# Batch 0 by token slot, its u made transposed in PSUM, and three-chunk weight pieces in a gated-recurrence and mixer kernel

## The chip, the cores and the metric

The kernel runs on one core of one Trainium2 chip. The metric is device time in microseconds (us) of one execution, lower is better; the time before is the median of three runs.

## The reference

Two parts follow one another. The first is a recurrence per batch and head over 768 tokens, with a state of 48 by 48; its output, with heads side by side, is x of 768 tokens by 384 channels. The second is a mixer: two matmuls over tokens with a residual give u, two matmuls over channels with a residual give the output.

```python
B, H, S, D = 4, 8, 768, 48
for t in range(S):
    state = alpha[:, :, t, :, None] * state + einsum('bhd,bhe->bhde', k[:, :, t], v[:, :, t])
    y[:, :, t] = einsum('bhd,bhde->bhe', q[:, :, t], state)
x = y.transpose(0, 2, 1, 3).reshape(B, S, H * D)                 # 4, 768, 384
h = maximum(x.transpose(0, 2, 1) @ w_tok1, 0) @ w_tok2           # w_tok1 768 x 256, w_tok2 256 x 768
u = x + h.transpose(0, 2, 1)
out = u + maximum(u @ w_ch1, 0) @ w_ch2                          # w_ch1 384 x 1536, w_ch2 1536 x 384
```

All inputs and the output are float32; the kernel computes in bf16 with float32 sums in PSUM.

## The kernel before

**Attention.** Each batch is cut into three blocks of 256 tokens, numbered 0 to 11 over the four batches. A partition holds two neighbouring tokens of a block (the two token slots), so that one load per block and tensor (alpha, k, q, v) brings 384 KB in rows of 384 bytes. For a block, `ln` and cumulative sums on TensorE (`cum`, or `cumw` in blocks 0 to 2) and exponentials on ScalarE (`E`, `IE`) give decay factors; `kk` and `qq` scale k and q by them; `trk`/`trq` with `evk`/`evq` transpose them (through TensorE in blocks 0 to 5, through DMA transposes `dk` and `dq` in blocks 6 to 11). `G0_`, `G1_` are the score products of the two halves of 128 tokens, `mask0_`, `mask1_` mask them on VectorE into `gtm`, `K` is the product of k and v for the state, `s`, or `sa` and `sm`, update the state, `ia`/`ib` add the state's part to the output, `y` the part within the block, and `x0_`, `x1_` copy the result to x. Two of these steps need whole halves of 128 tokens on the partitions, so that `vs0_`, `vs1_`, `ka`, `kb` and `kc` copy 64 partitions each across the two slots. A second form of the block, by token slot, is in the code and unused (`SLOT = ()`): `gslot` and `maskslot` go by slot, `khalf` and `yslot` use 64 rows of the TensorE array at a time, and `kadd` adds the old state in PSUM by an identity matmul. It needs none of the five copies.

**Mixer.** Per batch: `t1` (12 matmuls of 384 columns) and `ht` (ReLU) are the first token layer, `t2` (12 matmuls) the second; `u` adds x on VectorE. The channel layers need u transposed (`ut`): batch 0 transposes on TensorE (`UP = (0,)`, operations `up` and `ut`), batches 1 to 3 by two DMA transposes `ux`. `c1` (72 matmuls, with ReLU `rt`) and `c2` (72 matmuls in 24 groups) are the channel layers, `o` adds u on VectorE, and `st` stores.

**Weights** come in 16 loads of 384 KB (`ldw`) and are cast to bf16 (`cw`): two pieces of w_tok1 (`wt1`), two of w_tok2 (`wt2`, 128 rows each), six of w_ch1 (`wc1`: 128 rows by 768 columns), six of w_ch2 (`wc2`). `c1` with the first six groups of 128 columns needs three `wc1` pieces, with the last six the other three.

**Order.** Nothing is scheduled on the chip by chance: a search with a cost model, run beforehand, left a written list (`ORDER`) of some 930 operations. The last letter of each is its engine: t TensorE, v VectorE (DVE), s ScalarE (ACT), g GpSimd (POOL), y SyncE (SP), the queue that issues all loads and DMA transposes. Each engine works through its operations in the list's order, so an operation that waits holds up all behind it on its engine. `BUFS` are the buffer numbers that belong to it. Operations named f1 to f12 are fillers: matmuls on zeros, in units of 512 columns, put where TensorE would wait. [...]

Around the change the list of before reads, from the last block of batch 0 to the first channel matmul (`c1_0_11_0`):

```
ia2t y0_2t x0_2s t1_0_0_1t t1_0_0_2t E3s t1_0_0_3t mask1_2v t1_0_1_3t ib2t y1_2t ldw_wc14y t1_0_1_4t
x1_2s t1_0_0_4t f1_t1_0_1_5t t1_0_1_5t ht_0_1v P4g cw_wt21s t1_0_0_5t ht_0_0s f3_t2_0_0t t2_0_0t t2_0_1t u_0_0v ln13s
r13s ldw_wc13y t2_0_2t u_0_1v t2_0_3t u_0_2v t2_0_5t lnP4s t2_0_4t u_0_3v u_0_5v u_0_4v up_0_0t cw_wc14s cw_wc13s
ldw_wc15y up_0_1t ld_qt3y k0a3g kk3g cum4t trk3t cw_wc15g ut_0_0v up_0_2t ut_0_2v ut_0_1s c1_0_11_0t c1_0_8_0t IE4s
```

Of the kernel before, what the change touches and what calls it, by code (L numbers as in the profile page):

```python
# [9 lines left out]
BF16 = mybir.dt.bfloat16  # L10
# [84 lines left out]
B, H, S, D = 4, 8, 768, 48  # L95
# [6 lines left out]
UP = (0,)  # L102
# [11 lines left out]
SLOT = ()  # L114
# [6 lines left out]
def build(g):  # L121
# [194 lines left out]
    def mixer(b):  # L316
# [27 lines left out]
        uts = []
        if b in UP:
            for p in range(3):
                bank = V("one")
                o = P.op(f"up_{b}_{p}", pe([128] * 6), m0 + (3900 + 340 * p) * sc, writes=[bank],
                         reads=list(dict.fromkeys([us[2 * p][0], us[2 * p + 1][0]])),
                         preds=[us[2 * p][1], us[2 * p + 1][1]],  # L350
                         emit=lambda e, p=p, bank=bank: g.utr(bank, [us[2 * p][0], us[2 * p + 1][0]], p))
                uts.append(P.op(f"ut_{b}_{p}", either(dve(768, True), act(768)), m0 + (3950 + 340 * p) * sc, writes=[ut],
                                reads=[bank], preds=[o], emit=lambda e, p=p, bank=bank: g.utev(e, ut, bank, p)))
        else:
            for half in range(2):
                uts.append(P.op(f"ux_{b}_{half}", {"SP": (1240.0, 1240.0)}, m0 + (3900 + 500 * half) * sc, writes=[ut],
                                reads=[us[3 * half][0]], preds=[us[3 * half + i][1] for i in range(3)],
                                emit=lambda e, half=half: g.uxbar(ut, us[3 * half][0], half),
                                dma=("x", 1450.0, 1180.0, 480.0)))
        rts = []  # L360
        for mc in range(NDC):
            rt = V("rt")
            ro = []
            for half in range(2):
                bank = V("one")
                o = P.op(f"c1_{b}_{mc}_{half}", pe([384] * 3), m0 + (4900 + 975 * mc + 487 * half) * sc, writes=[bank],
                         reads=[ut], preds=(uts[0:2 + half] if b in UP else [uts[half]]) + [wl[("wc1", p)] for p in ((0, 1, 2) if mc < 6 else (3, 4, 5))],
# [5 lines left out]
        for i in range(NS):  # L373
            hold = 4000.0 if (i >= NS - 3 and b < B - 1) else 0.0
            cuts = [(0, HD // 2), (HD // 2, HD)] if (b, i) == LAST else [(0, HD)]
            for ci, (ca, cz) in enumerate(cuts):
# [3 lines left out]
                for q4 in range(4):  # L380
                    pp = []
                    for mc in range(3 * q4, 3 * q4 + 3):
# [6 lines left out]
                          reads=[bank, us[i][0]], preds=[prev],  # L389
# [20 lines left out]
ld_at1y ld_at0y ln1s ln0s f8_cumw1t f1_cumw1t cumw1t IE1s cumw0t IE0s ld_vt0y E0s vb0g vs0_0g vs1_0v ld_kt0y kk0v  # L410
f8_trk0t f1_trk0t trk0t E1s ld_qt0y qq0v ka0s kb0s kc0v f1_trq0t trq0t ld_kt1y kk1v K0t evq0s s0_0v ld_vt1y vb1s
f1_trk1t trk1t ld_at2y evk0v ln2s f2_G0_0t G0_0t ld_qt1y ka1g sa1_0v f4_cumw2t cumw2t mask0_0v vs0_1s kb1g kc1g vs1_1s
K1t sm1_0g qq1v sa0_1v sm0_1v G1_0t ld_kt2y IE2s E2s trq1t evq1s ib0t mask1_0v f3_y1_0t y1_0t y0_0t evk1v G0_1t sa1_1v
ld_qt2y x1_0s mask0_1v G1_1t ld_vt2y x0_0s vb2s kk2g trk2t kc2s ldw_wt10y qq2g cw_wt10s f2_ia1t ia1t mask1_1v evk2s
trq2t ld_at3y vs1_2g ldw_wt11y evq2v ib1t y1_1t y0_1t vs0_2g ldw_wt21y sm1_1g P3g K2t sa0_2v sm0_2g x0_1s t1_0_0_0t
f1_G0_2t G0_2t ldw_wt20y G1_2t cw_wt20g t1_0_1_0t mask0_2v x1_1s t1_0_1_1t ld_at4y ld_kt3y t1_0_1_2t lnP3s cum3t
cw_wt11s IE3s ia2t y0_2t x0_2s t1_0_0_1t t1_0_0_2t E3s t1_0_0_3t mask1_2v t1_0_1_3t ib2t y1_2t ldw_wc14y t1_0_1_4t
x1_2s t1_0_0_4t f1_t1_0_1_5t t1_0_1_5t ht_0_1v P4g cw_wt21s t1_0_0_5t ht_0_0s f3_t2_0_0t t2_0_0t t2_0_1t u_0_0v ln13s
r13s ldw_wc13y t2_0_2t u_0_1v t2_0_3t u_0_2v t2_0_5t lnP4s t2_0_4t u_0_3v u_0_5v u_0_4v up_0_0t cw_wc14s cw_wc13s
ldw_wc15y up_0_1t ld_qt3y k0a3g kk3g cum4t trk3t cw_wc15g ut_0_0v up_0_2t ut_0_2v ut_0_1s c1_0_11_0t c1_0_8_0t IE4s  # L420
c1_0_11_1t rt_0_8_0v rt_0_11_0v ldw_wc11y q0r3g qq3g c1_0_9_1t rt_0_9_1v ln14s kb3s c1_0_10_0t cw_wc11s c1_0_9_0t
rt_0_9_0v rt_0_11_1v E4s c1_0_7_0t c1_0_10_1t c1_0_7_1t ldw_wc10y r14s cw_wc10s rt_0_10_1v trq3t evk3s rt_0_7_0v
ldw_wc12y ld_vt3y cw_wc12g c1_0_2_0t c1_0_0_1t ka3g rt_0_7_1s c1_0_8_1t rt_0_10_0v vb3v vs1_3g vs0_3g rt_0_0_1v
rt_0_2_0v evq3s ld_at5y ld_qt4y c1_0_1_1t rt_0_8_1v c1_0_3_0t kc3s K3t P5g c1_0_4_1t rt_0_3_0s rt_0_1_1s q0r4g G0_3t
ld_kt4y qq4g s0_3v ln15s G1_3t sa1_3v c1_0_2_1t rt_0_2_1s mask0_3v lnP5s c1_0_1_0t c1_0_5_1t rt_0_5_1s rt_0_1_0s r15s
mask1_3v ldw_wc21y cw_wc21s k0a4g ldw_wc20y c1_0_6_1t rt_0_6_1v c1_0_4_0t kk4v ldw_wc22y c1_0_5_0t c1_0_0_0t cw_wc22s
rt_0_4_0v rt_0_0_0v cw_wc20g rt_0_4_1s c1_0_6_0t rt_0_6_0v c1_0_3_1t trq4t rt_0_3_1v cum5t trk4t ld_kt5y k0a5g
ldw_wc23y rt_0_5_0s c2_0_3_0t c2_0_5_0t evq4s kb4s evk4v ld_qt5y G1_4t mask1_4v G0_4t ld_vt4y c2_0_0_0t IE5s c2_0_0_1t
ka4g cw_wc23s c2_0_3_1t kc4s sm1_3g E5s mask0_4v ib3t y1_3t ldw_wc24y cw_wc24s c2_0_5_1t vb4g vs1_4s x1_3s ia4t
ldw_wc25y vs0_4g cw_wc25s ld_at6y y0_3t kk5v c2_0_3_2t y0_4t q0r5v trk5t evk5s qq5v K4t c2_0_0_2t sa0_4v c2_0_0_3t P6v  # L430
x0_3s ld_at7y sm0_4g o_0_0v trq5t x0_4s sa1_4v P7g evq5s lnP6s c2_0_5_2t c2_0_5_3t ld_vt5y vb5g c2_0_4_0t c2_0_4_1t
ld_kt7y kc5g G1_5t G0_5t lnP7s o_0_5v ib4t y1_4t vs1_5s mask1_5v t1_1_1_0t t1_1_1_1t sm1_4g x1_4s c2_0_4_2t c2_0_3_3t
vs0_5s ld_at8y t1_1_1_2t st_0_5s K5t mask0_5v sa0_5v sm0_5v cum6t t1_1_0_0t ld_kt6y k0a6g t1_1_0_1t ld_qt6y c2_0_2_0t
ln17s ld_qt7y ia5t y0_5t x0_5s IE6s kk6g ib5t y1_5t ln16s E6s t1_1_0_2t x1_5v t1_1_0_3t t1_1_1_3t cum7t E7s o_0_3v
t1_1_1_4t t1_1_1_5t r16s ld_kt8y q0r6g ld_vt6y dk6y P8g ht_1_1v lnP8s t1_1_0_4t t1_1_0_5t c2_0_2_1t c2_0_2_2t ln18s
ht_1_0v t2_1_1t u_1_1v t2_1_2t t2_1_0t t2_1_4t u_1_2v u_1_0v ux_1_0y c2_0_1_0t c2_0_1_1t vb6s IE7s qq6v r17s t2_1_3t
# [529 lines left out]
```

## Time and profile before

| | us |
|---|---|
| three runs | 163.32, 163.56, 162.62 |
| median | 163.32 |
| span of the profiled execution, first to last instruction | 160.5 |
| TensorE busy (matmuls) | 154.6 |
| VectorE, ScalarE, GpSimd busy | 114.9, 97.8, 80.8 |

The profiled execution has no time of its own beside its span; the median of the runs lies 2.8 us above that span. In the profile PE is TensorE's matmul side, PEld its weight loads, DVE, ACT and POOL the Vector, Scalar and GpSimd engines, SPq the issuing queue of SyncE. Matmuls are pipelined: a single one of 384 columns is shown with 0.33 us, a row of them advances by about half of that each. In rows of the timeline the first number is the start in us from the first instruction, the second the duration, and a bracket tells the idle time ahead and what ended it; in groups stand busy us and mean ns.

### The profile page before, as it was taken

What the parts mean: (1) busy time and instruction counts of PE and PEld (TensorE: products, weight loads), DVE (VectorE), ACT (ScalarE), POOL (GpSimd) and SP (SyncE); (2) the same over time, 40 slices, a digit from 0 to 9 for tenths busy, and PEclk for the clock granted to TensorE, in tenths of its full rate; (3) what the DMA queues carried; (4) which work ended last, traced back from release to release, by engine and by line L of the source; (5) the groups of instructions that cost most, each with busy time, mean ns of one, the idle gap of its engine ahead of it and who ended that gap; (6) DMA issues with size and microseconds to landing.
All of it is one profiled execution on the core that took longest, in us unless ns stands there. A gap on an engine that the chain in (4) does not pass through costs nothing.

```text
span 160.5 us, 3971 instructions
## 1 busy us (share of the span) xinstructions
PE 154.6 (96%) x1563; PEld 97.1 (60%) x1563; DVE 114.9 (72%) x206; ACT 97.8 (61%) x179; POOL 80.8 (50%) x94
## 2 busy tenths in 40 slices
PE   7999989999999999999999999999999999999992
PEld 2545565766667676666667666566567665665661
DVE  6099994979889787989969758795886762464222
ACT  3789999998899955897563583269832203343000
POOL 5205897695973649389778852699523000000000
PEclk9999999999999999999999999999999999999999
DMA  4999999999999999999989999989701235111133
GB/s 122 320 324 317 317 374 311 339 333 306 316 347 324 275 278 272 210 228 319 241 202 298 239 315 204 217 196 134 196 21 62 87 79 169 49 49 53 49 129 116
DMA packets 76130, 35.05 MB, mean 218 GB/s; under 512 B 70352, under 2 KB 74320, under 8 KB 76112
## 3 DMA queue, kind: packets, MB, share of 16 engines
q1 hardware_dynamic: 73808, 31.76, 74.1%
q10 hardware_dynamic: 2304, 3.05, 5.3%
q8 instruction: 12, 0.20, 0.5%
q14 instruction: 6, 0.05, 0.1%
HBM read 25.17 MB, written 4.72 MB: 186 GB/s over the span
## 4 chain that ended last, share of the span: by engine, by line
PE 61%; DMA 12%; DVE 6%; ACT 6%; SPq 6%; POOL 4%; issue 3%; DVEq 0%; POOLq 0%
PE ps L907 22%; PE ps L902 21%; PE ps L643 11%; DMA in<-in_v_dram 6%; SPq L584 6%; DMA out_dram<-o 4%; PE ps L878 3%; PE ps L883 2%; DMA ut<-u 2%; DVE pkk L700 2%; DVE gtm L770 1%; PE ps L712 1%; DVE rt L875 1%; POOL vb L746 1%; POOL pkq L700 1%
## 5 line engine op out<-in xcount | busy, mean ns | idle before, releaser
L907 PE MATMUL ps<-wc,rt 128*128 128x384 bf16 (+1 forms) x300 | 52.4, 319 | 0.0
L902 PE MATMUL ps<-ut,wc 128*128 128x384 bf16 x288 | 50.3, 326 | 0.1
L902 PEld LDWEIGHTS <-wc 128*128 128x128 bf16 x288 | 27.1, 98 | 17.9 <-DMA ut<-u 0.6
L907 PEld LDWEIGHTS <-rt 128*128 128x128 bf16 x300 | 27.8, 98 | 16.0
L873 ACT ACTIVATE rt<-ps 128x384 bf16<-128x384 f32 x47 | 21.4, 492 | 23.6 <-PE ps L902 23.3
L875 DVE TENSOR_SCALAR rt<-ps 128x384 bf16<-128x384 f32 x49 | 25.6, 551 | 9.1 <-PE ps L902 8.9
L770 DVE TENSOR_TENSOR gtm<-ps,mk 128x1024 bf16<-128x1024 f32 x24 | 28.5, 1218 | 3.1 <-PE ps L643 2.8
L911 DVE TENSOR_TENSOR o<-ps,u 128x384 f32<-128x384 f32 (+1 forms) x25 | 13.2, 536 | 12.6 <-PE ps L907 10.1
L700 POOL TENSOR_TENSOR pkk<-in,IE 128x768 bf16<-128x768 f32 x8 | 14.5, 1817 | 3.3 <-DVE ss L844 2.3
L745 ACT CAST x<-ps 128x384 bf16<-128x384 f32 x20 | 9.2, 479 | 11.1 <-PE ps L643 9.5
L887 DVE TENSOR_TENSOR u<-ps,x 128x384 bf16<-128x384 f32 x24 | 12.0, 550 | 3.1 <-PE ps L883 2.5
L746 POOL CAST vb<-in 64x384 bf16<-64x384 f32 (+1 forms) x14 | 8.3, 594 | 10.4 <-DMA in<-in_v_dram 4.7
L692 POOL TENSOR_TENSOR in<-in,in 128x384 f32<-128x384 f32 x8 | 8.0, 1000 | 10.5 <-DVE u L887 3.8
L643 PE MATMUL ps<-rt 128*128 128x512 bf16 (+1 forms) x29 | 12.1, 515 | 1.1 <-DVE rt L541 1.1
L745 ACT CAST vb<-in 64x384 bf16<-64x384 f32 (+1 forms) x18 | 11.4, 634 | 0.8 <-DMA in<-in_v_dram 0.3
L700 POOL TENSOR_TENSOR pkq<-in,E 128x768 bf16<-128x768 f32 x6 | 10.9, 1818 | 0.6 <-DMA tpk<-pkq 0.3
L878 PE MATMUL ps<-x,wt 128*128 128x384 bf16 x48 | 11.0, 325 | 0.0
L844 POOL TENSOR_TENSOR ss<-tmp,E 128x384 bf16<-128x384 f32 x10 | 8.3, 833 | 4.2 <-DVE in L628 3.9
L841 DVE TENSOR_TENSOR tmp<-ps,ss 128x384 f32<-128x384 f32 x16 | 8.8, 552 | 1.8 <-PE ps L643 0.6
L883 PE MATMUL ps<-ht,wt 128*128 128x384 bf16 x48 | 9.1, 326 | 0.0
L643 PE MATMUL ps<-vb,gtm 128*128 128x48 bf16 x192 | 8.2, 183 | 0.2 <-DVE gtm L770 0.2
L643 PE MATMUL ps<-tpq,tpk 48*64 48x128 bf16 (+1 forms) x288 | 7.9, 218 | 0.4 <-POOL tpq L746 0.3
(94 smaller groups left out, 207.6 us busy)
## 6 DMA issues: line engine op xcount, KB each, us to landing
in<-in_alpha_dram SPq DMA_DIRECT2D x12, 384.0 KB, 5.1
in<-in_v_dram SPq DMA_DIRECT2D x12, 384.0 KB, 5.6
in<-in_k_dram SPq DMA_DIRECT2D x12, 384.0 KB, 5.2
in<-in_q_dram SPq DMA_DIRECT2D x12, 384.0 KB, 5.5
in<-in_moe_w_ch_dram SPq DMA_DIRECT2D x12, 384.0 KB, 5.9
out_dram<-o ACTq DMA_DIRECT2D x15, 192.0 KB, 1.8
in<-in_moe_w_tok_dram SPq DMA_DIRECT2D x4, 384.0 KB, 6.0
out_dram<-o SPq DMA_DIRECT2D x8, 192.0 KB, 2.2
```

Source lines behind the costliest of these rows:

```text
L643: return self.pe.matmul(out, lhsT=lhsT, rhs=rhs, start=start, stop=stop, skip_group_check=True)
L700: self.shared(self.eng[e].tensor_tensor(self.t(dst)[:, :, h0:h1, 0:D], self.t(src)[:, h0:h1].rearrange("p h s d -> p s h d"), bass.AP(tens ...
L745: return self.act.copy(d, s)
L770: self.nc.vector.tensor_tensor(self.t(gtm)[:, hf, :, :], self.pair(gp).rearrange("p a (j t) -> p (a j) t", t=128), bass.AP(tensor=m.tensor ...
L873: self.act.activation(d, s, AF.Relu)
L875: self.nc.vector.tensor_scalar_max(d, s, 0.0)
L878: self.pe.matmul(self.bank(bank)[:, 0:HD], lhsT=self.wt1[:, kc, m * 128 : m * 128 + 128], rhs=self.t(x), start=(kc == 0), stop=(kc == NS - 1))
L883: self.pe.matmul(self.bank(bank)[:, 0:HD], lhsT=self.wt2[:, kc, i * 128 : i * 128 + 128], rhs=self.t(hts[kc]), start=(kc == 0), stop=(kc = ...
L887: self.nc.vector.tensor_tensor(self.t(u)[:, i % 3], self.bank(bank)[:, 0:HD], self.t(x), ALU.add)
L902: self.pe.matmul(self.bank(bank)[:, 0:HD], lhsT=self.wc1[:, kc, mc * 128 : mc * 128 + 128], rhs=self.t(ut)[:, 3 * half : 3 * half + 3, kc, ...
L907: self.pe.matmul(self.bank(bank)[:, 0 : cz - ca], lhsT=self.t(rts[mc][0])[:, i * 128 : i * 128 + 128], rhs=self.wc2[:, mc, ca:cz], start=( ...
L911: self.nc.vector.tensor_tensor(self.t(o)[:, ca:cz], self.bank(bank)[:, 0 : cz - ca], self.t(u)[:, i % 3, ca:cz], ALU.add)
```

## The change

1. `SLOT = (0,1,2)`: the three blocks of batch 0 use the form by token slot. The copies `ka`, `kb`, `kc`, `vs` of these blocks go, and their state additions are made by TensorE (`A`).
2. `UDIR = (0,)` in place of `UP`: batch 0's second token layer is computed transposed (`tt`), after identity matmuls (`xa`) have put x, transposed, into the same PSUM bank; six copies (`ut`) of 384 columns give ut directly. u in its natural layout, which `o` needs, comes back from ut by two DMA transposes on the SP queue (`un_0_1`, `un_0_0`).
3. Weight pieces: a `wc1` piece is now all 384 rows by 256 columns, so that a channel group needs one piece; a `wt2` piece is all 256 rows by 384 columns. Each load still moves 384 KB; its rows are 1,024 and 1,536 bytes long in place of 3,072.
4. `ORDER` and `BUFS` are new as a whole, for all batches. Fillers go from 36 units to 27.

```diff
-UP = (0,)
+UP = ()
+UDIR = (0,)
-SLOT = ()
+SLOT = (0,1,2)
...
+        if b in UDIR:
+            ut, us, uts = V("ut"), [], []
+            for half in range(2):
+                evs = []
+                for j in range(NM):
+                    bank = V("one")
+                    tx = x[3 * half : 3 * half + 3]
+                    xa = P.op(f"xa_{b}_{half}_{j}", pe([128] * 3), ..., writes=[bank],
+                              reads=[v for v, _ in tx], preds=[o for _, o in tx], ...)
+                    o = P.op(f"tt_{b}_{half}_{j}", pe([384] * 2), ..., writes=[bank],
+                             reads=[h for h, _ in hts], preds=[h for _, h in hts] + [xa, wl[("wt2", half)]], ...)
+                    evs.append(P.op(f"ut_{b}_{half}_{j}", either(act(384), dve(384)), ...,
+                                    writes=[ut], reads=[bank], preds=[o], ...))
+                uts.append(evs)
                 u = V("u")
+                un = P.op(f"un_{b}_{half}", {"SP": (1240.0, 1240.0)}, m0 + 6000 * sc, writes=[u], reads=[ut], preds=evs,
+                          emit=lambda e, u=u, half=half: g.unat(u, ut, half), dma=("x", 1450.0, 1180.0, 480.0))
+                us += [(u, un)] * 3
...
-                         ... [wl[("wc1", p)] for p in ((0, 1, 2) if mc < 6 else (3, 4, 5))],
+                         ... [wl[("wc1", mc // 2)]],
...
-                          reads=[bank, us[i][0]], preds=[prev],
+                          reads=[bank, us[i][0]], preds=[prev, us[i][1]],
...
-            self.gated(dma(t, self.w[1][128 * piece : 128 * piece + 128, :]), op)
+            w = self.w[1].rearrange("(c p) m -> p c m", p=128)
+            self.gated(dma(t.rearrange("p (c m) -> p c m", c=2), w[:, :, HD * piece : HD * piece + HD]), op)
         elif nm == "wc1":
-            c, h = piece % 3, piece // 3
-            self.gated(dma(t, self.w[2][128 * c : 128 * c + 128, 768 * h : 768 * h + 768]), op)
+            w = self.w[2].rearrange("(c p) m -> p c m", p=128)
+            self.gated(dma(t.rearrange("p (c m) -> p c m", c=3), w[:, :, 256 * piece : 256 * piece + 256]), op)
...
+    def xadd(self, bank, xs, j):
+        for i, x in enumerate(xs):
+            self.mm(self.bank(bank)[:, i * 128 : i * 128 + 128], self.t(x)[:, j * 128 : j * 128 + 128], self.idn, i == 0, False)
+
+    def tok2t(self, bank, half, j, hts):
+        for kc in range(NDT):
+            self.mm(self.bank(bank)[:, 0:HD], self.t(hts[kc])[:, j * 128 : j * 128 + 128],
+                    self.wt2[:, half, kc, :], False, kc == NDT - 1)
+
+    def utev3(self, e, ut, bank, half, j):
+        self.copy(e, self.t(ut)[:, 3 * half : 3 * half + 3, j, :], self.bank(bank)[:, 0:HD].rearrange("p (i t) -> p i t", i=3))
+
+    def unat(self, u, ut, half):
+        self.nc.sync.dma_start_transpose(self.t(u).rearrange("p i (j c) -> p (i j) c", j=NM),
+                                         self.t(ut)[:, 3 * half : 3 * half + 3].rearrange("p i j t -> p (i j t)"))
```

The new list, in the two places that the prediction follows: from the scores of the last block of batch 0 to the first channel matmul (`c1_0_4_1`), and from the last channel weights to batch 1's second token layer (`t2_1_0`). Loads leave in the list's order; `ldw_wc12` is the 20th, `ldw_wc24` the 39th, `ld_at7` the 43rd.

```
ld_qt2y G0_1t x0_0s mask0_1v ld_kt2y ld_vt2y qq2g f3_trq2t trq2t evq2s ldw_wt10y A1_1t s1_1v G1_1t mask1_1v kk2g
ld_at3y ln13s f2_trk2t trk2t ia1t evk2v f2_G1_2t G1_2t mask1_2v P3g ib1t y1t cw_wt10s r13s lnP3s G0_2t ia2t mask0_2v
vb2g K2t A0_2t x0_1s x1_1s cum3t IE3s ldw_wt20y cw_wt20g t1_0_1_0t t1_0_1_1t s0_2v E3s xa_0_0_1t ib2t y2t t1_0_0_0t
t1_0_1_2t x0_2v ld_at4y P4g lnP4s ldw_wt11y x1_2s ln14s r14s ld_qt3y t1_0_0_1t cw_wt11g t1_0_1_3t t1_0_0_2t t1_0_0_3t
q0r3v qq3v t1_0_1_4t ldw_wt21y xa_0_0_2t t1_0_1_5t ht_0_1s t1_0_0_4t t1_0_0_5t xa_0_1_1t ht_0_0s cum4t cw_wt21v trq3t
evq3v tt_0_1_1t xa_0_1_0t tt_0_1_0t ut_0_1_0s ut_0_1_1s xa_0_0_0t IE4s xa_0_1_2t tt_0_1_2t ut_0_1_2v ldw_wc12y
tt_0_0_0t ut_0_0_0s cw_wc12g ld_kt3y k0a3g kk3v tt_0_0_1t tt_0_0_2t ut_0_0_1v c1_0_4_1t rt_0_4_1v c1_0_5_1t ld_at5y
...
x1_4v G0_5t ldw_wc23y G1_5t cw_wc23g mask1_5v mask0_5v ldw_wc24y cw_wc24g c2_0_5_2t c2_0_2_2t ldw_wc25y c2_0_3_1t
sm1_4g K5t sa0_5v sm0_5v ld_at8y P8g ld_kt7y cw_wc25s c2_0_2_3t un_0_1y c2_0_3_2t ld_at7y P7v ia5t y0_5t x0_5s
t1_1_0_0t t1_1_0_1t c2_0_5_3t o_0_5v ld_at6y ld_kt6y ib5t y1_5t t1_1_1_2t x1_5s t1_1_0_2t t1_1_1_3t P6g t1_1_0_3t
t1_1_0_4t t1_1_1_4t t1_1_1_5t ld_qt6y t1_1_0_5t c2_0_4_0t c2_0_4_1t ht_1_0v ln17s lnP7s ld_kt8y ld_vt7y ht_1_1s
t2_1_0t u_1_0v ln16s t2_1_2t t2_1_5t cum7t t2_1_1t u_1_5v u_1_1v k0a7g u_1_2v c2_0_3_3t r16s q0r6v IE7s kk7g lnP6s
```

More of the change, by code (lines that the diff above doesn't have):

```diff
@@ L366, in mixer @@
                 o = P.op(f"c1_{b}_{mc}_{half}", pe([384] * 3), m0 + (4900 + 975 * mc + 487 * half) * sc, writes=[bank],
-                         reads=[ut], preds=(uts[0:2 + half] if b in UP else [uts[half]]) + [wl[("wc1", p)] for p in ((0, 1, 2) if mc < 6 else (3, 4, 5))],
+                         reads=[ut], preds=(uts[half] if b in UDIR else uts[0:2 + half] if b in UP else [uts[half]]) + [wl[("wc1", mc // 2)]],
                          emit=lambda e, mc=mc, half=half, bank=bank: g.ch1(bank, ut, mc, half))
@@ L415 @@
[L415 to L424, printed above, removed]
@@ L613, in wcast @@
         elif nm == "wt2":
-            d = self.wt2[:, piece, :]
+            d, t = self.wt2[:, piece], t.rearrange("p (c m) -> p c m", c=2)
         elif nm == "wc1":
-            c, h = piece % 3, piece // 3
-            d = self.wc1[:, c, 768 * h : 768 * h + 768].rearrange("p (q r k) -> p q r k", q=3, r=2)
-            t = t.rearrange("p (q k r) -> p q r k", q=3, r=2)
+            d = self.wc1[:, :, 256 * piece : 256 * piece + 256].rearrange("p c (r k) -> p c r k", r=2)
+            t = t.rearrange("p (c k r) -> p c r k", c=3, r=2)
         else:
@@ L882, in tok2 @@
         for kc in range(NDT):
-            self.pe.matmul(self.bank(bank)[:, 0:HD], lhsT=self.wt2[:, kc, i * 128 : i * 128 + 128], rhs=self.t(hts[kc]),
+            self.pe.matmul(self.bank(bank)[:, 0:HD], lhsT=self.wt2[:, i // 3, kc, i % 3 * 128 : i % 3 * 128 + 128], rhs=self.t(hts[kc]),
                            start=(kc == 0), stop=(kc == NDT - 1))
```

176 lines of the change are left out of this document (93 added, 83 removed), and 22 rows, old and new, of the table BUFS.

## The prediction

> **What bounds the kernel now.** I read the page first, then the windows, the chain of waits, and the timeline of the first 60 us.
>
> ```profile
> span 160.5 us, 3971 instructions
> PE 154.6 (96%) x1563; PEld 97.1 (60%) x1563; DVE 114.9 (72%) x206; ACT 97.8 (61%) x179; POOL 80.8 (50%) x94
> ...
> PEclk9999999999999999999999999999999999999999
> DMA  4999999999999999999989999989701235111133
> ```
>
> TensorE is busy for 96% of the span at full granted clock, and the DMA engines are full for the first half. The windows say where TensorE still waits:
>
> ```profile
> 20.00:24.00 4.00, 3.53 (x58) 2.39 (x57) 3.88 (x5) 3.74 (x8) 3.81 (x6) 1.00 1.08 375
> ...
> 40.00:50.00 10.00, 9.93 (x111) 6.60 (x111) 8.79 (x12) 9.11 (x18) 8.26 (x10) 1.00 1.02 332
> ...
> 100.00:110.00 10.00, 9.93 (x102) 5.99 (x101) 8.13 (x14) 5.42 (x13) 7.88 (x7) 1.00 0.97 189
> 110.00:120.00 10.00, 9.72 (x142) 6.40 (x141) 7.50 (x11) 6.99 (x12) 5.44 (x6) 1.00 0.53 122
> ```
>
> (Busy us and instructions of PE, PEld, DVE, ACT, POOL; clock; DMA share; GB/s.) Ahead of 24 us all engines are nearly full. From 40 us on TensorE misses 0.07 + 0.07 + 0.28 us in these windows, and next to nothing in the others until the last store. The boundary is the first matmul of batch 0's channel mixer (c1); rows of the timeline, then the last three of the chain:
>
> ```profile
> 25.33 0.33 PE L643 MATMUL ps<-ss,tpq 128*128 128x96 bf16 x4
> ...
> 25.58 0.37 PE L643 MATMUL ps<-vb,gtm 128*128 128x48 bf16 x8
> ...
> 25.99 0.48 ACT L745 CAST x<-ps 128x384 bf16<-128x384 f32 x1
> ...
> 27.10 0.49 ACT L873 ACTIVATE ht<-ps 128x384 bf16<-128x384 f32 x1
> ...
> 27.73 2.28 PE L883 MATMUL ps<-ht,wt 128*128 128x384 bf16 x12
> 29.85 0.83 PE L894 MATMUL ps<-idn,u 128*128 128x128 bf16 x12
> 31.76 4.55 PE L902 MATMUL ps<-ut,wc 128*128 128x384 bf16 x27
> ...
> 147.62 9.79 PE ps L907 x72
> 157.42 0.02 issue
> 157.44 0.36 DVE o L911
> ```
>
> So the last x of batch 0 is there at 26.47, c1 begins at 31.76, and TensorE then works until 157.4 with almost no gap. Those 125.6 us are the same matmuls in both kernels: behind its first c1 the old order has all slot work of batches 1 to 3 but cum3, cum4 and trk3, the new one all but cum3, cum4 and trq3, and both transposes are eight of 128 columns. **The end therefore moves by what c1's start moves, plus the change in TensorE's waits behind it.** Fillers, of which 36 units of 512 columns become 27, stand only ahead of c1 in both; they fill waits, and dropping them alone gains nothing.
>
> **When inputs arrive.** Loads leave one queue in a written order.
>
> ```profile
> 4.28 0.84 ACT L637 ACTIVATE la<-in 128x768 bf16<-128x768 f32 x1 [2.19 <-DMA in<-in_alpha_dram]
> ...
> 30.16 0.88 POOL L746 CAST wc<-in 128x768 bf16<-128x768 f32 x1 [0.36 <-DMA in<-in_moe_w_ch_dram]
> ...
> 48.50 1.39 POOL L746 CAST vb<-in 128x768 bf16<-128x768 f32 x2 [0.29 <-DMA in<-in_v_dram]
> ```
>
> Consumers that waited for the 1st, 22nd and 37th load start at 4.28, 30.16 and 48.50: 1.23 us a load over either stretch, so load k can be used at 4.28 + 1.23 (k-1). The new order keeps this pace if its weight pieces do. They turn rows of 3,072 bytes (wc1, wt2) into 1,024 and 1,536.
>
> ```profile
> in<-in_moe_w_ch_dram SPq DMA_DIRECT2D x12, 384.0 KB, 5.9
> ...
> in<-in_moe_w_tok_dram SPq DMA_DIRECT2D x4, 384.0 KB, 6.0
> ```
>
> wt1 has rows of 1,024 bytes already and is half of the second row, which lands in 6.0 us against 5.9. I cost the pieces at nothing; the bounds are 0 and 0.1 each, 0.6 over six.
>
> **The change, part by part.** *Attention of batch 0.* Per-slot form drops 13 half-swapping copies (ka, kb, kc, vs) and replaces four DVE additions by TensorE's.
>
> ```profile
> L770 DVE TENSOR_TENSOR gtm<-ps,mk 128x1024 bf16<-128x1024 f32 x24 | 28.5, 1218 | 3.1 <-PE ps L643 2.8
> L700 POOL TENSOR_TENSOR pkk<-in,IE 128x768 bf16<-128x768 f32 x8 | 14.5, 1817 | 3.3 <-DVE ss L844 2.3 <-PE ps L643 0.7
> L700 DVE TENSOR_TENSOR pkq<-in,E 128x768 bf16<-128x768 f32 x6 | 5.7, 955 | 0.3 <-POOL in L628 0.2
> L841 DVE TENSOR_TENSOR tmp<-ps,ss 128x384 f32<-128x384 f32 x16 | 8.8, 552 | 1.8 <-PE ps L643 0.6 <-POOL ss L844 0.5
> L745 ACT COPY kt<-pkk 64x384 bf16<-64x384 bf16 x6 | 3.1, 509 | 0.5 <-POOL pkk L700 0.4
> L745 ACT COPY tpk<-ps 128x1024 bf16<-128x1024 bf16 x3 | 3.0, 1010 | 0.0
> L746 DVE COPY tpk<-ps 128x1024 bf16<-128x1024 bf16 x3 | 2.0, 679 | 0.0
> L746 POOL CAST vb<-in 128x768 bf16<-128x768 f32 x4 | 3.3, 823 | 4.7 <-DMA in<-in_v_dram 4.7
> ```
>
> But the new order puts five of six k and q products (qq0, qq1, kk1, qq2, kk2) on POOL, at 1.82 where DVE takes 0.96. q0 is load 5 (9.2), q1 load 7 (11.66). qq0 ends at 11.0; qq1 and kk1 at 15.3. From there: eight transposes (twelve took 0.83 above) 0.6 and ACT's evk1 1.0 to 17.0, the vb1 cast (16.1), state and first products to 17.5. DVE then has, in its order, s0_1, mask0_1, s1_1, mask1_1, evk2, two masks, s0_2: 3 x 0.55 + 4 x 1.22 + 0.68 = 7.2, and about 0.4 waiting for the score matmuls between: 25.1. The last inter and y matmuls take 0.6 (the rows of 25.33 and 25.58), the evacuation x 0.55 like any DVE operation of 384 columns: **26.3, against 26.47**. POOL's own side (qq2 and kk2 to 19.8) ends earlier than evk2 needs it. What the dropped copies free, the slower products take back. If DVE's copies and not POOL's products set the pace, this is up to 1 us better; the floor is k2, load 11 (16.6).
>
> *From x to c1.* Before: first-layer matmuls, ht, twelve second-layer matmuls, six DVE additions, transposes, evacuation: 31.76 - 26.47 = 5.3. After, x joins by identity matmuls (xa, of which most come early), and 384-column evacuations give ut directly. On DVE, behind x0_2, stand q0r3, qq3 and the cast of wt2's second half (cw_wt21), for which tt waits (groups by form, then two rows of the chain):
>
> ```profile
> L696 DVE TENSOR_TENSOR in<-in,lf 128x384 f32<-128x384 f32 x3 | 1.7, 552 | 0.1
> L746 DVE CAST vb<-in 128x768 bf16<-128x768 f32 x1 | 0.6, 550 | 0.0
> ...
> 62.80 1.30 PE ps L883 x8
> 73.18 0.57 PE ps L643 x32
> ```
>
> 26.3 + 0.55 + 0.96 + 0.55, with 0.1 between, is 28.5. ACT's two ht, behind ln14 and r14, are ready then too (0.5 each from 26.4). The first three tt are six matmuls of 0.163, with three xa of about 0.17 between: 1.5, then 0.55 and 0.2 of latency for the evacuation: 30.7; meanwhile the other three tt run, 1.0 from 30.0. **c1 starts at 31.1, 0.65 earlier.** ut's evacuations hide behind tt. wc12, load 20 (27.7) with 0.88 for its cast, is ready at 28.6.
>
> *Packed halves.* The last row above is a pair of score products in 64x64 tiles, 32 in 0.57 us: side by side, as the new form needs. [...] I bound the packed form by 0 and 1.2 on c1's start (the last slot's matmuls at twice their time: 0.57 for the scores, 0.4 for y as in the row of 25.58, 0.2 for the state) and take 0, since the row shows packing at work.
>
> *Weights behind c1.* The tightest piece is wc24, now load 39: 51.0 + 0.9 for the cast. Its user c2_0_5_2 has 21 us of TensorE work between it and the first c1 (24 c1 and 5 c2 groups of three matmuls, 29 x 0.49 = 14.2; 6.8 of slot work, of which five blocks of eight transposes are 2.3, three score pairs 2.0 and the rest states, inters and y at 0.2 to 0.35): 31.1 + 21 = 52.1. Hidden by 0.2. Before, wc24 was load 38.
>
> *The new transposes* un_0_1 and un_0_0 bring u back for the output addition.
>
> ```profile
> 64.68 1.29 SPq L729 DMA_TRANSPOSE ut<-u  x1
> ...
> ut<-u SPq DMA_TRANSPOSE x6, 3.0
> ```
>
> un_0_1 goes ahead of the loads of alpha 7 and 6. It holds the queue 1.3 (bounds 0 and its landing time, 3.0), so alpha 7, load 43, comes at 55.9 + 1.3 = 57.2. On DVE P7 waits for it; behind P7 stand o_0_5 (which waits for un_0_1 itself) and ht_1_0, for which t2_1_0 waits: 57.2 + 3 x 0.55 + 0.2 = 59.1. TensorE reaches t2_1_0 27.4 us after c1's start (37 groups of 0.49, 12 t1 of 0.163, 7.4 of attention): 58.5. **A new wait of 0 to 0.6; I take 0.3.** un_0_0 stands behind batch 1's first ut transpose, ahead of its second, which has over 2 us of matmuls to hide in.
>
> *Sum.* -0.65 + 0.3 = -0.35, so 160.15 in place of 160.5. The median of the three runs, 163.32, lies 2.8 above the profiled span, which I keep; the runs spread from 162.62 to 163.56, so 0.5% (0.8 us) is about what can be told from no change. **162.9 us**, within 0.5%.
>
> **Rivals.** *Faster:* my head is too slow, DVE and ACT being freer than I count, and c1 starts when its weights allow, near 29. Then the weights bind: wc24 at 51.9 and 104.6 us of matmuls behind c2_0_5_2 (125.6 - 21) end at 156.5, 0.9 earlier; with the 0.4 of waits in the windows gone also, 1.3 earlier: 162.0. For it: 24 us of crowded engines lose 13 copies of half a microsecond. Against it: the five products on POOL. Chance 0.34.
>
> *Slower:* the wait at t2_1_0. If un_0_1 lands like a load in a full queue (the rows above: 5.9, not 3.0), o_0_5 stalls DVE, and with it ht_1_0 and batch 1's second layer; later stages have no slack to recover it. It decides once un_0_1 or alpha 7 lands after 57.4 and costs all beyond that: 162.97 + 2.9 = 165.9 at its worst, 164.4 at half. For it: DMA is full there. Against: alpha 7 comes behind it anyway. Chance 0.14.
>
> *It does not pack:* the halves run one after another, 1.2 on c1's start: 164.2. The score pair above speaks against it. Chance 0.09.
>
> *The clock falls* in the head, where windows now show 1.00, since fewer fillers bridge its waits. From the last filler (near 22) to c1 some 6 us of matmuls would take twice as long, half of it hidden: +3, 166. Chance 0.05. [...]
>
> **How the numbers follow.** No measurable change 0.38, faster 0.34, slower 0.14 + 0.09 + 0.05 = 0.28. The range goes from the faster case with a little more (161.6) to half-way into the slower one (164.9); within 0.5% alone is 162.5 to 164.1.
>
> **What would show it.** c1's first matmul at 31.1 in the timeline (29 for the faster rival, over 32 for the unpacked one); POOL's last product ending near 20; ht_1_0's wait, and DVE waiting for a DMA near 57, for the new wait; PE's busy time lower by what fillers go, the windows from 40 us as full as before. I am wrong if TensorE shows gaps of over 1 us behind c1, or if the load pace leaves 1.23.

## The result, and the profile after

The changed kernel is slower: 168.41 us median of four runs (168.02 to 170.34) against 163.44 (162.62 to 164.42) for the kernel before on the same chip, a ratio of 1.0354 with a 95% interval of 1.0275 to 1.0433. The prediction was 162.9, its range ended at 164.9. Ratios here and below leave out executions more than 1.5% above the fastest of the same kernel; for one kernel (no_un1) these are five of eight, 166.7 to 168.7 us, so that its ratio stands on three.

The page of the changed kernel (busy us and share, then slices of the span, then the chain of waits by engine):

```profile
span 168.6 us, 4178 instructions
PE 154.8 (92%) x1675; PEld 97.0 (58%) x1675; DVE 112.0 (66%) x198; ACT 94.0 (56%) x178; POOL 76.4 (45%) x83
...
PEclk9999999999999999999999999999999999999999
...
PE 40%; DMA 27%; SPq 16%; POOL 8%; issue 4%; DVE 2%; ACT 2%; POOLq 0%; DVEq 0%; ACTq 0%
```

TensorE is busy as long as before (154.8 us against 154.6), at full clock; the span is 8 us longer. So TensorE waits more, and the chain that ends last runs through transfers and SP's own queue for 43% of the span, where it was 18%. Rows of its timeline (start, duration; in brackets the idle time ahead and what ended it):

```profile
32.46 1.14 PE L943 MATMUL ps<-ut,wc 128*128 128x384 bf16 x6
...
52.02 5.16 SPq L938 DMA_TRANSPOSE u<-ut  x1
...
61.54 0.56 DVE L653 TENSOR_TENSOR in<-in 128x384 f32<-128x384 f32 x1 [2.59 <-DMA in<-in_alpha_dram]
...
63.09 1.14 PE L908 MATMUL ps<-ht,wt 128*128 128x384 bf16 x6 [1.03 <-DVE ht L900]
...
79.06 1.14 PE L943 MATMUL ps<-ut,wc 128*128 128x384 bf16 x6 [1.95 <-DVE rt L900]
```

L938 is un_0_1. It stands on SP for 5.16 us, not 1.3; alpha 7 behind it is late, DVE waits for it, and TensorE waits at t2_1_0: the place that the slower rival named. But the row at 79.06 is a longer gap far behind it, and c1's first matmul is at 32.46, not at 31.1.

This execution was the slowest of the four (170.34). One figure serves for comparing profiles: **the gap sum**, for each matmul behind c1's first the time to the next start, less the median of its form, added up where it is over 60 ns. It is 3.4 us before and 10.8 here; what is left of TensorE's time behind c1 is 122.0 us in both, so the matmuls are the same, as the prediction had it. It is a figure of one execution each; ratios rest on several.

### The profile page after: what moved, and what is told of

It reads as the page before. It is cut to its first block, busy times and chain, and to the rows that moved or that the text cites. A ratio compares the mean times of both kernels' runs of the same rounds, so it can differ in the third digit from the quotient of the medians.

```text
span 168.6 us, 4178 instructions
## 1 busy us (share of the span) xinstructions
PE 154.8 (92%) x1675; PEld 97.0 (58%) x1675; DVE 112.0 (66%) x198; ACT 94.0 (56%) x178; POOL 76.4 (45%) x83
## 4 chain that ended last, share of the span: by engine, by line
PE 40%; DMA 27%; SPq 16%; POOL 8%; issue 4%; DVE 2%; ACT 2%; POOLq 0%; DVEq 0%; ACTq 0%
PE ps L948 17%; PE ps L943 14%; SPq L607 7%; DMA tpk<-pkq 6%; DMA in<-in_alpha_dram 5%; SPq L629 5%; PE ps L668 4%; DMA in<-in_k_dram 4%; DMA in<-in_v_dram 4%; DMA in<-in_moe_w_ch_dram 3%; DMA in<-in_q_dram 3%; SPq L938 3%; PE ps L903 2%; PE ps L908 2%; POOL pkq L725 2%
## 5 line engine op out<-in xcount | busy, mean ns | idle before, releaser
L898 ACT ACTIVATE rt<-ps 128x384 bf16<-128x384 f32 x56 | 25.5, 490 | 24.9 <-PE ps L943 22.6
L900 DVE TENSOR_SCALAR rt<-ps 128x384 bf16<-128x384 f32 x40 | 21.0, 553 | 12.4 <-PE ps L943 12.3
L795 DVE TENSOR_TENSOR gtm<-ps,mk 128x1024 bf16<-128x1024 f32 x18 | 21.1, 1216 | 1.8 <-PE ps L668 1.8
L725 POOL TENSOR_TENSOR pkq<-in,E 128x768 bf16<-128x768 f32 x9 | 16.3, 1811 | 11.5 <-DMA in<-in_q_dram 8.9
L912 DVE TENSOR_TENSOR u<-ps,x 128x384 bf16<-128x384 f32 x18 | 9.4, 553 | 4.0 <-PE ps L908 3.3
L770 ACT CAST vb<-in 64x384 bf16<-64x384 f32 (+1 forms) x14 | 8.7, 624 | 4.9 <-DMA in<-in_v_dram 4.7
L653 POOL TENSOR_TENSOR in<-in 128x384 f32<-128x384 f32 x7 | 7.0, 1001 | 9.6 <-DMA in<-in_alpha_dram 4.0
L668 PE MATMUL ps<-rt 128*64 128x384 f32 (+1 forms) x21 | 9.2, 540 | 1.1 <-DVE rt L564 1.1
L668 PEld LDWEIGHTS <-tpk 48*64 48x64 bf16 (+1 forms) x336 | 6.0, 104 | 6.3 <-issue 4.5
L668 PE MATMUL ps<-vb,gtm 128*128 128x48 bf16 (+1 forms) x240 | 8.1, 182 | 0.0
```

The source lines that it names most:

```text
L668: return self.pe.matmul(out, lhsT=lhsT, rhs=rhs, start=start, stop=stop, skip_group_check=True)
L725: self.shared(self.eng[e].tensor_tensor(self.t(dst)[:, :, h0:h1, 0:D], self.t(src)[:, h0:h1].rearrange("p h s d -> p s h d"), bass.AP(tens ...
L770: return self.act.copy(d, s)
L795: self.nc.vector.tensor_tensor(self.t(gtm)[:, hf, :, :], self.pair(gp).rearrange("p a (j t) -> p (a j) t", t=128), bass.AP(tensor=m.tensor ...
L898: self.act.activation(d, s, AF.Relu)
L900: self.nc.vector.tensor_scalar_max(d, s, 0.0)
```

## The experiments

**The same kernel again.**

> The changed kernel itself once more, for a second profile of it. Both theories: about 168.4 us. If the slow pace of the loads (12th landed at 19.5 us, 28th at 40.1) and the 5.2 us that the queue stood at un_0_1 belong to the kernel and not to one execution, they are seen again within 0.5 us, and c1 starts near 32.5.

168.57 and 168.82 us, ratio 1.0351 [1.0299, 1.0403]. Timeline of this second profile (span 166.9), the head first:

```profile
26.04 0.56 DVE L771 CAST x<-ps 128x384 bf16<-128x384 f32 x1 [0.92 <-PE ps L668]
...
27.62 0.87 ACT L898 ACTIVATE ht<-ps 128x384 bf16<-128x384 f32 x2
...
31.10 1.14 PE L943 MATMUL ps<-ut,wc 128*128 128x384 bf16 x6
...
49.24 5.10 SPq L938 DMA_TRANSPOSE u<-ut  x1
...
58.91 0.56 DVE L653 TENSOR_TENSOR in<-in 128x384 f32<-128x384 f32 x1 [2.23 <-DMA in<-in_alpha_dram]
...
60.46 1.14 PE L908 MATMUL ps<-ht,wt 128*128 128x384 bf16 x6 [0.68 <-DVE ht L900]
```

The late head is not a property of the kernel: here the last x ends at 26.6, c1 starts at 31.10. The hold at un_0_1 is there again (5.10), and the gap sum is 10.5. Against the profile of before that is -0.66 from c1 and +7.04 from gaps, together the 6.4 us by which the spans differ. The span of before used here, 160.5, lies at the short end (most executions of it on the chip of this run have 161.2 to 161.5), so that up to 1 us of the 7.04 is that choice; the ratio stands for 5.7 us. Windows of before and then of this run show where the gaps lie (busy us of PE is the second number):

```profile
70.00:80.00 10.00, 10.00 (x114) 6.35 (x113) 9.41 (x17) 7.44 (x15) 9.21 (x7) 1.00 1.11 255
80.00:90.00 10.00, 10.00 (x151) 6.64 (x150) 8.60 (x13) 5.01 (x11) 7.80 (x9) 1.00 0.95 246
90.00:100.00 10.00, 10.00 (x92) 6.42 (x90) 6.82 (x14) 6.09 (x13) 5.22 (x6) 1.00 1.04 261
```

```profile
70.00:80.00 10.00, 8.30 (x52) 4.70 (x51) 6.87 (x14) 5.59 (x11) 6.41 (x6) 1.00 1.00 243
80.00:90.00 10.00, 8.70 (x122) 5.44 (x121) 7.61 (x13) 6.59 (x13) 5.42 (x5) 1.00 1.21 226
90.00:100.00 10.00, 8.49 (x144) 5.98 (x142) 7.96 (x13) 2.70 (x7) 5.65 (x6) 1.00 1.16 276
```

4.5 us go between 70 and 100, where the kernel before has none to lose. Its DMA transposes on SP (ns: least, median, most) and then those of this run:

```profile
L729 SPq DMA_TRANSPOSE ut<-u x6: 1272/1300/1887, 64.7 to 131.2; - x6
...
L725 SPq DMA_TRANSPOSE tpk<-pkk x6: 1231/1278/1905, 62.9 to 109.2; - x6
L725 SPq DMA_TRANSPOSE tpk<-pkq x6: 1232/1244/1867, 66.7 to 112.0; - x6
```

```profile
63.61 3.12 SPq L754 DMA_TRANSPOSE ut<-u  x1
...
70.38 2.85 SPq L750 DMA_TRANSPOSE tpk<-pkq  x1
...
76.80 3.44 SPq L750 DMA_TRANSPOSE tpk<-pkk  x1
...
88.54 2.41 SPq L750 DMA_TRANSPOSE tpk<-pkq  x1
```

The 1.3 us is the price of a transpose with no load ahead of it: in all profiles kept, the transposes on SP for which every earlier load had landed took 1.23 to 1.78 us. In the packet records of this run, every one that takes over 2.2 us has a load ahead that is still to land, and ends 0.7 to 1.4 us before that load's last packet: un_0_1 at 54.35, k7's at 55.06; dk7 at 80.23, q8's at 81.25. SP stands there and issues nothing else. The reverse does not hold: dk9, issued at 100.92 with a load ahead that landed only at 105.15, stood 1.36 us, and nine more in the other profiles stood 1.2 to 1.7 us with 3.35 to 3.8 still to go. What decides between the two is not shown.

**Without the un transposes, with long rows, and both.** no_un drops un_0_1 and un_0_0 (batch 0's output is permuted); rows_long fetches wc1 and wt2 as before (weights permuted); both does the two.

```diff
-                us += [(u, un)] * 3                # un_0_1y, un_0_0y out of ORDER
+                us += [(ut, evs)] * 3
...
-            self.gated(dma(t.rearrange("p (c m) -> p c m", c=3), w[:, :, 256 * piece : 256 * piece + 256]), op)
+            self.gated(dma(t, self.w[2][128 * c : 128 * c + 128, 768 * h : 768 * h + 768]), op)
```

> The changed kernel without un_0_1 and un_0_0: the output addition of batch 0 reads ut as it lies, so batch 0's output is permuted. Queue theory (the new transposes hold SP's queue for 5 us and what stands behind them comes late): the 1.2 us gap at t2_1_0 near 62 us goes and those near 71 and 77 us shrink; 164.5 to 166. Pace theory (the weight pieces with short rows slow all loads): the loads before 50 us stay as late as they are; alpha 7 comes 4 us earlier, but the gaps before 46 us and most of those after 70 us stay; 167 or more.

> The changed kernel with the wc1 and wt2 pieces fetched as before, in rows of 3,072 bytes; the weights so land permuted. Pace theory: no issue of a weight load takes over 2 us, the 28th load lands near 37 instead of 40, c1 starts near 31.3, the gaps at 35.9, 37.3 and 44.5 us go; 165 to 166.5. Queue theory: the un transposes still hold the queue and the waits behind 61 us stay; 167.5 or more.

> Both edits together: no un transposes and long rows. If the two theories hold all of the loss, the time is at most that of before (162.5 to 163.5), since head and order are then as predicted. If the new order itself has no slack (a third theory: c1 late and waits on banks and evacuations that no transfer causes), it stays above 165 with gaps behind c1 of 2 us or more.

Ratios 1.0163 [1.0067, 1.0259], 1.0241 [1.0191, 1.0290] and 1.0161 [1.0093, 1.0228]; gap sums 6.0, 8.3, 6.3. Without un 3 us come back, with long rows 1.8, with both no more than without un alone. But alpha 7 does not come the expected 4 us earlier. In no_un its load stands where un_0_1 stood, and is held there itself (this row is alpha 7 with 3.90 us and alpha 6 with 1.01):

```profile
49.91 5.01 SPq L594 DMA_DIRECT2D in<-in_alpha_dram  x2
```

The two loads take 5.0 us of the queue here; un_0_1 and the two took 6.4 (49.24 to 55.60). So un_0_1 adds about 1.4: alpha 7 lands at 58.79 with it and at 57.37 without, and with the long rows at 57.07 and 56.12. (In no_un1 below, on another chip, it landed at 56.03; these are single profiles.) The short rows make it 1.3 to 1.7 later in the same four. What un adds to TensorE's waits is mostly further on: of the 4.4 us by which the gap sums of again and no_un differ, 0.8 stand at t2_1_0; the two largest gaps that no_un lacks are 1.5 at 82.6, for dk7 (landed 84.15, in no_un 79.53), and 1.65 at 94.4, behind dq8 (94.73 against 89.75). How 1.4 us at alpha 7 grow to almost 5 there is not traced.

Neither theory holds all of it: 2.6 us are left, though c1 is as early as predicted (31.1). What is left in both, from its timeline:

```profile
72.41 0.56 DVE L939 TENSOR_TENSOR o<-ps,ut 128x384 f32<-128x384 f32 x1 [1.58 <-DMA out_dram<-o]
...
73.39 0.49 ACT L884 ACTIVATE rt<-ps 128x384 bf16<-128x384 f32 x1 [0.94 <-DVE o L939]
...
73.49 0.81 PE L929 MATMUL ps<-ut,wc 128*128 128x384 bf16 x4 [1.25 <-DVE rt L886]
```

o_0_2 takes the buffer of o_0_4, whose store ACT issues late, among its rt; DVE stands 1.58 us, the rt behind it frees a bank late, TensorE waits. The longest gap of the changed kernel (the row at 79.06 in its first profile) is this wait too: DVE's o stood 2.47 us there for a store, and 2.21 at 74.98 in the second profile. The second gap (1.24 us at 92) is dq8's: two loads stand ahead of it on SP.

**Each addition alone, on the kernel before.** before_un adds the two transposes of ut at like places in the old list; before_pieces takes the new pieces alone; before_un_pieces takes the two together.

```diff
+                P.op(f"un_{b}_{half}", {"SP": (1240.0, 1240.0)}, 0, reads=[ut], preds=[],
+                     emit=lambda e, half=half: g.unat(half, ut))
```

> The kernel before, with two transposes of ut added on SP's queue, one behind the load kt7 and one behind the second transpose of batch 1's u; nobody reads what they bring. Queue theory: the first holds the queue for 3 us or more, everything behind it comes so much later, and the kernel is 1 to 3 us slower. If a transpose holds the queue only 1.3 us, as the prediction had it: within 0.5 us of before.

> The kernel before with the new weight pieces alone (wc1 in rows of 1,024 bytes, wt2 in rows of 1,536), in its own list. Pace theory (short rows slow all loads): the last of wc1's pieces lands 1 us or more later, 1 to 1.5 us slower. If the rows cost nothing: within 0.5 us of before, and earlier if its first c1 waited for a piece.

> The kernel before, in its own list, with both of the change's additions to the queue: the two transposes of ut (nobody reads what they bring) and the new weight pieces. If these two are the change's loss and the new list and the slot form are worth little: 167.5 to 168.5, as the changed kernel. If the list loses 2 us of its own: 165.5 to 166.5.

Ratios 1.0218 [1.0113, 1.0323], 1.0087 [1.0044, 1.0129] and 1.0208 [1.0163, 1.0253]. The transposes cost 3.6 us on a list that they were never planned into, where nobody reads their results; the pieces cost 1.4 alone and nothing beside the transposes. Timeline of before_un_pieces, then of before_pieces:

```profile
52.55 3.06 SPq L901 DMA_TRANSPOSE ut<-ut  x1
...
64.24 2.22 SPq L728 DMA_TRANSPOSE tpk<-pkk  x1
...
69.81 2.61 PE L910 MATMUL ps<-ut,wc 128*128 128x384 bf16 x15 [1.46 <-DMA ut<-u]
```

```profile
31.58 0.87 POOL L746 CAST wc<-in 128x768 bf16<-128x768 f32 x1 [1.82 <-DMA in<-in_moe_w_ch_dram]
...
32.50 4.56 PE L902 MATMUL ps<-ut,wc 128*128 128x384 bf16 x27 [0.82 <-POOL wc L746]
```

The added transpose holds the queue 3.06 us, dk6 behind the delayed loads 2.22 (1.33 in the kernel before), and batch 1's first ux lands 1.5 us late for c1. The piece that was cast at 30.16 is cast at 31.58, and c1 starts 0.74 later, because in that list c1 waits for its weights; in the changed kernel it does not. The median of before_un_pieces, 166.36, lies where it was expected if the new list loses 2 us of its own (1.0208 here, 1.0351 for the changed kernel).

**One of the two transposes.** no_un1 drops un_0_1 and keeps un_0_0 (half of batch 0's output is permuted).

> The changed kernel without un_0_1 alone (the output addition of batch 0's second half reads ut, that half permuted); un_0_0 stays. Queue theory: un_0_1 is the one that stands 5.1 us ahead of alpha 7, un_0_0 holds the queue for only 1.4; so 2 to 3 of the 3 us that both together are worth come back: 165.7 to 166.7. If the two cost by their traffic alone, half comes back: 167.2.

1.0072 [1.0034, 1.0111]; span 162.5, gap sum 6.0, both as in no_un. As far as three executions tell, un_0_1 carries what the two cost, and un_0_0, behind a transpose, next to nothing.

**From another queue.** un_act has ACT issue them (`self.nc.scalar.dma_start_transpose`).

> The changed kernel with un_0_1 and un_0_0 issued by ACT instead of SP, un_0_0 a little earlier, where ACT waits; a right output. Queue theory (a transpose stands at the head of SP's queue until the loads ahead of it have nearly landed, and the loads behind it start into an empty queue): ACT has no loads ahead, its issue takes 1.3 us, alpha 7 is issued 4 us earlier, the gap at t2_1_0 goes; 165.5 to 166.5, as without the un transposes. Traffic theory (the transposes cost by the bytes and packets that they move, whichever queue issues them): 168 or more.

1.0538 [1.0427, 1.0650]: slower still. The 165.5 to 166.5 of the queue theory is missed; the 168 or more of the traffic theory is met in number, but not for its reason, since the bytes are those of the changed kernel.

```profile
53.74 1.34 ACTq L921 DMA_TRANSPOSE u<-ut  x1
...
60.73 0.56 DVE L935 TENSOR_TENSOR o<-ps,u 128x384 f32<-128x384 f32 x1 [2.25 <-DMA u<-ut]
...
69.08 3.12 SPq L737 DMA_TRANSPOSE ut<-u  x2
...
73.01 8.16 PE L926 MATMUL ps<-ut,wc 128*128 128x384 bf16 x39 [2.86 <-DMA ut<-u]
```

The issue takes 1.34 us, as expected, but it comes 4.5 us later than SP's did (49.24): on ACT it stands behind the cast of wc25, which waits for its load. The transfer then lands 6.9 us after its issue, much as from SP (7.4), so at 60.64 and not at 56.64, and DVE waits for it in o_0_5. SP gains little: in un_0_1's place alpha 7's load stood 3.89 us, as in no_un.

un_0_0 was moved ahead in the list too, before batch 1's first ux, and that ux is issued only at 69.08, when SP had been idle since 63.6. Its u was written by 64.6. The semaphore that SP waited for until 69.02 is the one that un_0_0's transfer, issued by ACT at 63.26, had filled at 69.00, so the wait is one that the program holds. Why the program holds it is not shown; with it, the second queue brought no overlap here: the ux was issued 5.82 us after un_0_0's issue and 0.08 after its landing.

Behind TensorE's 2.86 us of waiting its granted clock falls. In the profiles of before and of the changed kernel it does not, as long as matmuls run. (The window's clock is the third number from the end.)

```profile
70.00:80.00 10.00, 7.14 (x34) 3.79 (x34) 4.28 (x8) 3.81 (x9) 3.12 (x4) 0.83 0.98 215
```

From 72.98 to 76.39 it was 0.5, and matmuls of 384 columns came 0.32 us apart in place of 0.163. That cost 1.65 us, about half of the 3 us by which un_act is slower than the changed kernel by the ratios.

**The list.** The re-orderings move operations without changing them:

```diff
-... dk6y ld_at9y ld_qt8y dk7y dq6y st_0_0y ld_vt8y ld_at11y dk8y ld_at10y ld_kt9y dq8y ...   (SP)
+... dk6y dk7y ld_at9y ld_qt8y dq6y dk8y st_0_0y ld_vt8y dq8y ld_at11y ld_at10y ld_kt9y ...
-... st_0_3s ... st_0_4s ... st_0_5s   (ACT, among rt)
+st_0_5s behind ht_1_1s, st_0_3s behind vb7s, st_0_4s behind IE8s
```

> The changed kernel without the un transposes (the output addition of batch 0 reads ut, its output permuted) and with two stretches of the list re-ordered: dk7, dk8 and dq8 go ahead of the loads that stand before them on SP's queue, and ACT issues the stores of o_0_5, o_0_3 and o_0_4 as soon as each is written. List theory (what is left after no_un is the new list's placing of transposes behind fresh loads and of stores behind other work): the 1.4 us gap near 74 us and those of 1 us or more near 92 go; 162 to 163, the prediction's 162.9. If the rest is not the list: 164.3 or more, as without the re-ordering.

> The same re-ordering with the un transposes kept: a right output. List theory: the gaps near 74 and 94 us shrink, the one at t2_1_0 (0.8 to 1.2 us) stays, since un_0_1 still holds the queue; 165 to 166.5. If un_0_1's 5 us decide all that follows: 168 and more, as without the re-ordering.

> The same re-ordering without the un transposes and without the identity matmuls (batch 0's output permuted): what the list is worth by itself. List theory: 162 to 163, the prediction's 162.9. Otherwise 164.5 or more.

> The same with the re-ordering of before (dk7, dk8 and dq8 ahead of loads, three stores early) and, new, dk9 ahead of the loads q10 and v10, behind which it stood 4.2 us while the transposes of batch 2's u waited for it (a 2.1 us gap at 104 us). List theory: no gap of over 1 us is left behind c1; 162.5 to 163.5, level with before. If the list moves the wait on once more: 165 or more, with one new gap.

Ratios 1.0152 [1.0071, 1.0232], 1.0406 [1.0279, 1.0533], 1.0315 [1.0186, 1.0445] and 1.0567 [1.0422, 1.0711]: no gain is shown, and where a ratio is higher, its interval meets that of the kernel it starts from. Of order_no_un:

```profile
95.96 4.16 SPq L730 DMA_TRANSPOSE tpk<-pkk  x1
...
100.22 3.25 SPq L734 DMA_TRANSPOSE ut<-u  x2
...
104.41 1.15 PE L923 MATMUL ps<-ut,wc 128*128 128x384 bf16 x6 [1.91 <-DMA ut<-u]
```

The gap at 74 us is gone, 0.85 is left at 92, and one of 2.1 us (by start times) stands at 104: dk9, which the list leaves behind the loads q10 and v10, now comes up right after them and holds the queue 4.16 us, with batch 2's ux behind it. order2_no_un moves dk9 too, and its largest gaps are 0.9 to 1.2 us at 95 and 99; but in its profile c1 starts at 32.77, as late as in the first profile of the changed kernel, and why is not shown. The next three start from both and change less: the stores alone, then dq8 ahead of alpha 10 and k9, then dk9 too.

> The kernel without un transposes and with long rows (batch 0's output and the weights permuted), and with the stores of o_0_5, o_0_3 and o_0_4 issued as soon as each is written, nothing else re-ordered. List theory: its 1.4 us gap at 73.5 us, where o_0_2 waited on DVE for st_0_4 to land, goes and nothing takes its place: 164.0 to 164.5 after 165.7. If the list gives it back later: 165.5 or more, the gap near 92 us larger.

> As both_stores (no un, long rows, three early stores; batch 0's output and the weights permuted), with dq8 moved ahead of the loads alpha 10 and k9, which it followed on SP's queue: there it was issued at 83.05, held the queue 2.5 us and landed only near 89.6, and TensorE waited 2 us for the copy made from it. List theory: this gap goes and nothing takes its place: 162.5 to 163.3, level with before. If the list gives it back: 164 or more, with one new gap of over 1 us.

> The same and dk9 ahead of the loads q10 and v10. List theory: a few tenths below both_dq8, if the transposes of batch 2's u wait behind dk9 there; otherwise the same.

1.0074 [1.0031, 1.0117], 1.0112 [1.0053, 1.0170] and 1.0107 [1.0034, 1.0180]. The early stores are worth 1.4 us by these ratios (their interval meets that of both); the gap near 92 grows from 1.24 to 1.99, and with dq8 moved it goes and 1.73 appear at 103, behind dk9 once more. With all moves the kernel stays 1% over before.

**A version that computes all of the reference.** pe_add_order, on the list of order2_no_un, adds u by 18 identity matmuls into the last layer's banks; pe_half does so for the second half only, 9 matmuls, keeps un_0_0, and has the early stores and dq8 moved.

```diff
+        for j in range(NM if ut else 0):
+            self.mm(self.bank(bank)[:, j * 128 : j * 128 + 128], self.t(ut)[:, i, j, :], self.idn, False, j == NM - 1)
```

> Without un transposes, in a way that keeps the output right: u of batch 0 joins the last layer's sum by 18 identity matmuls of 128 columns on ut (some 1.0 us of TensorE), and the output is a copy out of PSUM; with the same re-ordering. List theory: 163.5 to 164.5, the kernel before plus 1.0 less the 0.65 of the earlier c1. If the rest is not the list: 166 or more.

> A right output without un_0_1: in batch 0's second half u joins the last layer's sum by 9 identity matmuls of 128 columns on ut (0.5 us of TensorE) and the output is a copy out of PSUM; un_0_0 and the short rows stay; three early stores, dq8 ahead of two loads. If un_0_1 and the two waits of the list are what is left: 163.0 to 164.5, some 4 us below the changed kernel. If not: 166 or more.

1.0320 [1.0228, 1.0412] and 1.0133 [1.0076, 1.0191]. pe_half recovers over half of the loss and is the best whole version with the new head; the kernel before remains faster.

## Why the prediction was wrong

- **The head was right.** x at 26.6 against 26.3, both ht by 28.5 as worked out, c1 at 31.10 against 31.1: the slower products on POOL (1.81 us each), the packed halves (32 matmuls of 64 rows in 0.57) and the identity matmuls (three in 0.17) came out as costed, and the unpacked rival (c1 over 32) fell. The two late heads (32.46 in the first profile, 32.77 in order2_no_un) are of single executions and unexplained.
- **The step that failed is the term "change in TensorE's waits behind c1": summed as +0.3, measured +7.0** (some 6.4 by the ratio). I compared one wait, at t2_1_0, and took the windows from 40 us on to stay as full as before. That wait came out at 0.8; the other 6 us, at 74, 82 and 94 us above all, were put at nothing without a reason.
- **"It holds the queue 1.3" was wrong as a hold.** The row it came from, at 64.68, had next to nothing left ahead (the last load's last packet came at 64.8); un_0_1 stands behind k7, whose last packet came 5.8 us after un's issue, and held SP 5.1 us. As a delay of alpha 7 it was about right, 1.0 to 1.4 on this chip, since a load in the same place is held 3.9: with the long rows alpha 7 landed at 57.07 and without un at 56.12, where the prediction had 57.2 and 55.9. The bound of 3.0 was a landing time from the same nearly idle queue.
- **The slower rival** named the place, at a chance of 0.14. One of its two conditions was met: alpha 7, used at 58.91, came after 57.4. Its reason was not what happened: un_0_1 itself landed at 56.64, before o_0_5 needed it. Its price of up to 2.9 was for this place, where 0.8 was lost; its own sentence, later stages have no slack, is what the rest bears out.
- **What the waits behind c1 are made of:** the un transposes, 3 us (no_un; on the old list 3.6, before_un); overlapping with these, the short rows (1.8 when they alone are taken out); and the new list's own, 2.6 us that are left without both though c1 is 0.65 earlier. In that list dk7, dk8 and dq8 stand right behind fresh loads and are held as long without un (3.48, 3.25 and 2.32 us in both) as with it (3.44, 2.95 and 2.41). One of the list's waits, stores against rt, is shown (both_stores); the remainder, about 1%, comes back at another transpose whenever one is moved, and which single order would end it stays open.
- **The clock rival** (0.05) did not come about: the granted clock was 1.00 from 20 to 32 us in the first profile of the changed kernel, as before. That fewer fillers would let it fall in the head was the author's estimate, and no run shows it. Matmuls at twice their time (0.32 us apart in place of 0.163, at a clock of 0.5) were seen in un_act, from 73 us on.
- **Weight pieces at 0, at most 0.6:** 1.4 us alone on the kernel before, 1.8 when taken out of the changed one, nothing to be seen where un is absent or has been added to the old list. The term is not zero, and not additive.
- **The offset of 2.8** between span and time was an artefact of setting a fast profile against a median: runs with their own spans show 1.7 (162.25 with 160.5, 168.57 with 166.9).

## What to carry to other kernels

A transpose on a queue that also carries loads stood here for 5.1 us, until the loads ahead of it had nearly landed (0.7 us before their last packet), and delayed all behind it; read such a price from the place where the transpose will stand, not from a row where the queue was nearly idle (1.29 us here), and ask what the next operation would pay in the same place: a load paid 3.9, and the net delay was 1.4. When the matmuls are the same, forecast every wait of the new order, not the one that the edit adds: here a start 0.65 us earlier was worth nothing, since 7.0 us of waits came behind it. Taking a wait out of a tight list shows its worth only by the end time, since the next one was standing right behind it.

## What the runs showed of the hardware

A DMA transpose of 128 x 1,024 or 128 x 1,152 bf16 was issued in 1.23 to 1.78 us with no load left to land, and behind loads in up to 5.16, the long ones (over 2.2) ending 1.0 to 2.4 us before the last load ahead landed; but one in the second profile took 1.36 us with 4.2 still to go. A load's issue in the same place was held too, 3.90 us in no_un.

From ACT's queue the same transfer was issued in 1.34 us and landed 6.9 us after its issue, from SP's 7.4 after. Here the second issuer brought 3.8 us less of issuing for this transfer (1.34 against 5.10), about the same time to land, and, since ACT came to it 4.5 us late, 2.25 us of waiting on DVE.

TensorE's granted clock was 0.5 for 3.41 us behind a wait of 2.86 us in un_act, and for the same time in un_act_order (72.89 to 76.30) and in both_stores (92.17 to 95.58). In both_dq8_dk9 TensorE waited 2.91 us ahead of 105.78, just as long as in un_act_order ahead of 73.04, and no fall came behind it: the length of one wait alone does not decide it, and what does is not shown.
